# Loads of one input issued from ScalarE's queue, five load buffers and a new hand order in a gated linear-attention and token-mixing kernel

## Chip, cores and metric

The kernel runs on one core of one Trainium2 chip. The metric is the device time of one execution in microseconds. The names of the engines are those of the profile: PE is TensorE's matmul side, PEld its weight loads, DVE is VectorE, ACT is ScalarE, POOL is GpSimd, SP is SyncE, which issues most transfers. ACTq and SPq are the queues of DMA-issuing instructions of ScalarE and SyncE.

## What is computed

Inputs r, k, v, w are (4, 8, 768, 48) in float32: 4 batches, 8 heads, 768 steps, 48 columns. The first stage is a recurrence over the steps, per batch and head, with a 48 x 48 state that decays by w; the second mixes the tokens of a batch with weights made from their own projections.

```python
for t in range(S):
    cur = np.einsum('bhd,bhe->bhde', u[None] * kt, vt)
    y[:, :, t] = np.einsum('bhd,bhde->bhe', rt, state + cur)
    state = wt[:, :, :, None] * state + np.einsum('bhd,bhe->bhde', kt, vt)
x = y.transpose(0, 2, 1, 3).reshape(B, S, H * D)      # (4, 768, 384)
W_tok = scale * np.einsum('bsd,btd->bst', x @ w_q, x @ w_k)
out = np.maximum(np.einsum('bst,btd->bsd', W_tok, x), 0) @ w_out
```

## The kernel before

The work is cut into 12 units of 256 steps, three to a batch, and a unit into two chunks c of 128 steps. The recurrence is written in its chunked form. For a unit n the steps are, with the names of the tiles that the profile shows:

- Four loads of 384 KB each (wg, kg, rg, vg; `load`, line 222), all from SP's queue, each into one of four buffers that take turns.
- Decays: ScalarE takes the logarithm of wg (lw, line 379); PE sums it along the steps with a triangular matrix CM (cw); ScalarE makes two exponentials of the sums, ep (line 423) and en (line 428).
- k and r are cast to bfloat16 (line 389) and transposed on PE with the identity ID; the transposed k is copied (ks), the products are qT (line 462), RT = r x ep (line 471, VectorE) and KT = k x en (line 476, VectorE or GpSimd). v is cast in quarters into VB (line 493). Vd (line 515, GpSimd) is v times the bonus dd.
- Per chunk: PE multiplies RT and KT to a 128 x 128 matrix A for each head; VectorE masks it to AM (line 535, 24 in all). PE transposes KT (kb), which is copied to kd; PE adds kd x VB to the old state (sn), and VectorE scales it to the new state SB (line 602), four tiles in turn.
- PE multiplies AM with VB (ya) and RT with the old state (yi); VectorE or ScalarE writes the result plus Vd as X (lines 668 and 670).
- X is transposed to XT, on PE for most units, by a DMA transpose from SP's queue for units 9 and 10 (`TURN`), and projected to QK (wk and wq). After the third unit of a batch, X and QK give a 64 x 384 matrix T, copied to TS. For each of the batch's units PE multiplies QK with TS (mx), an engine takes the relu into MX (lines 271 and 273), PE multiplies with wo (fp), an engine copies to os (line 259 or 265), and a store leaves from SP's queue (line 803).

The first and the last unit are split: their en, ep, RT, KT, kb and kd, and for the last also X, XT, QK, MX and os, are made in two halves, one for each chunk, so that the second half need not be waited for.

No scheduler decides the order. Every step is entered in a plan (`Plan.add`) with the engines that it may run on. Three tables written out by hand then fix everything: `ORDER` is the order in which the steps are issued, `WAYS` the engine of each step with a choice, and `BANKS` the PSUM bank of each intermediate result. An engine works through its instructions in that order; semaphores for the tiles are set from it. Each load takes one of eight DMA semaphores in turn, in the order of the program, and waits until the load that had it before has landed. Steps of kind z are matmuls on a zero tile that only keep PE at work. The numbers of buffers are in `RINGS` (line 193). A slot of RT, KT, ep or en holds one pair of heads hp and one chunk c, 128 columns, at place 2 x hp + c, so that the halves of a split unit lie interleaved in one tile:

```python
def plain(t, cs=(0, 1)):
    return view(t, cs[0] * C, [[1, 1024]] if len(cs) > 1 else [[U, NP], [1, C]])
```

All code below runs inside the function that sets up the tiles.

Of the kernel before, what the change touches and what calls it, by code (L numbers as in the profile page):

```python
# [32 lines left out]
class Plan:  # L33
# [86 lines left out]
]  # L120
WAYS = (
    "PPDDPDDDPDPDDPPPPPPDDPAPPEDddPPDAAcENDEDDAPEDdPAAEAEcEAEDAPPEDdAPAEDcNDEAAAAAAAADPPEAdPP"
    "AEAEEEAEDAPAcDPPADEAEcEAEAAPPcDdPPAEDcEAEADAAAAAAAPPcDdPPDEDccNDEAAPPcAdPPAeAEcNDEDAPPcD"
    "PPPDEDcEAEAAAADADAAPAcAdPPAEDEENDDPPcAdPPDeDccNDAPPcDPPPPDPPAcNDeAADNDEDDAADDDDDDAADAADN"
    "NNNNEEENNENNNENEEEENNEN"
)
# [16 lines left out]
def kernel(  # L143
# [12 lines left out]
    nc = tc.nc  # L156
# [703 lines left out]
```

## Time and profile before

| | |
|---|---|
| time, median of 3 runs (lowest, highest) | 101.48 us (100.37, 104.27) |
| time of the profiled execution | 99.53 us |
| its span, first to last instruction | 97.8 us |
| busy: PE, PEld, DVE, ACT, POOL | 87.7, 67.6, 81.7, 76.0, 68.1 us |
| granted clock of TensorE | 1.0 throughout |
| read, written | 19.66 MB, 4.72 MB |
| loads of 384 KB: from issue to landing, median by tile | 5.1 to 6.0 us |

The profiled execution lasts 1.73 us longer than its span; that is what lies before the first and after the last instruction. All times in the trace are counted from the start of the span. A row of a group names the line, engine, operation, output and inputs, and then the busy time in us, the mean duration of one in ns, the idle time of the engine just before, and what ended it. A row of a timeline has the start and the duration in us first; several alike are put together with their number behind an x, and the idle time before them stands in brackets. Two instructions that follow each other on VectorE or ScalarE overlap by some hundredths of a microsecond, so that they follow at a slightly shorter distance than their durations.

### The profile page before, as it was taken

The numbers are of one execution on the slowest core, as the hardware profiler recorded it, in microseconds if no ns is written. First come the engines' busy times: TensorE is split into PE (matmuls) and PEld (weight loads), VectorE is DVE, ScalarE is ACT, GpSimd is POOL, SyncE is SP. The second block draws the span as 40 slices with busy tenths as digits, with TensorE's granted clock in tenths as the row PEclk, the third lists the DMA queues.
The fourth block names the chain that finished last, engine by engine and source line by source line (L and its number), as shares of the span: only waits on it lengthen the run. The fifth ranks groups of instructions, "written<-read, shape, count | busy, mean of one in ns | idle before, by whom it ended". The sixth has DMA issues, their size and how long they took to land.

```text
span 97.8 us, 4074 instructions
## 1 busy us (share of the span) xinstructions
PE 87.7 (90%) x1710; PEld 67.6 (69%) x1713; DVE 81.7 (83%) x142; ACT 76.0 (78%) x112; POOL 68.1 (70%) x106
## 2 busy tenths in 40 slices
PE   4996888999889899999999999999999999998940
PEld 1354677878677798877788787897787776675410
DVE  5608989999999998999898999899998996384850
ACT  5237988889799799899999999869889856806610
POOL 6659758728799998767999998999968991000000
PEclk9999999999999999999999999999999999999999
DMA  1999999999999999999999999999913695928593
GB/s 29 304 323 325 325 325 299 222 292 315 287 306 247 227 287 215 304 270 245 303 301 308 277 300 294 311 323 248 289 57 132 195 153 150 397 83 322 215 319 112
DMA packets 54914, 25.03 MB, mean 256 GB/s; under 512 B 52592, under 2 KB 53744, under 8 KB 54896
## 3 DMA queue, kind: packets, MB, share of 16 engines
q1 hardware_dynamic: 54736, 24.58, 90.6%
q8 instruction: 13, 0.21, 0.8%
q10 hardware_dynamic: 160, 0.20, 0.6%
q14 instruction: 5, 0.04, 0.1%
HBM read 19.66 MB, written 4.72 MB: 249 GB/s over the span
## 4 chain that ended last, share of the span: by engine, by line
PE 42%; DMA 18%; POOL 18%; DVE 8%; issue 4%; ACT 3%; SPq 3%; POOLq 0%; DVEq 0%; ACTq 0%
PE PS L176 42%; DMA vg<-in_v_dram 12%; POOL VB L493 7%; POOL Vd L515 6%; DMA kg<-in_k_dram 6%; SPq L223 3%; DVE os L265 2%; POOL k L389 2%; POOL KT L476 2%; POOL r L389 2%; DVE RT L471 1%; ACT en L428 1%; DVE AM L535 1%; ACT ep L423 1%; DVE qT L462 1%
## 5 line engine op out<-in xcount | busy, mean ns | idle before, releaser
L535 DVE TENSOR_TENSOR AM<-PS,US 128x1024 bf16<-128x1024 f32 x24 | 28.8, 1218 | 1.0 <-PE PS L176 0.6
L493 POOL CAST VB<-vg 64x384 bf16<-64x384 f32 x42 | 21.1, 503 | 3.2 <-DMA vg<-in_v_dram 0.9
L515 POOL TENSOR_TENSOR Vd<-VB,dd 128x768 bf16<-128x768 bf16 (+1 forms) x14 | 18.0, 1292 | 1.6 <-DVE dd L265 1.1
L428 ACT ACTIVATE en<-PS,km 128x1024 bf16<-128x1024 f32 (+1 forms) x14 | 13.6, 989 | 2.4 <-PE PS L176 2.0
L423 ACT ACTIVATE ep<-PS,kp 128x1024 bf16<-128x1024 f32 (+1 forms) x14 | 13.8, 1003 | 1.4 <-PE PS L176 1.1
L176 PE MATMUL PS<-wo,MX 128*128 128x384 bf16 x72 | 13.5, 326 | 0.5 <-DVE MX L273 0.5
L176 PEld LDWEIGHTS <-KT 48*128 48x128 bf16 (+1 forms) x288 | 10.3, 95 | 3.9 <-issue 1.7
L389 POOL CAST k<-kg 128x768 bf16<-128x768 f32 x11 | 9.0, 824 | 4.5 <-DMA kg<-in_k_dram 4.3
L379 ACT ACTIVATE lw<-wg 128x768 bf16<-128x768 f32 x12 | 10.1, 844 | 2.2 <-DVE kd L230 2.1
L176 PE MATMUL PS<-RT,KT 48*128 48x128 bf16 x192 | 9.2, 217 | 1.2 <-DVE qT L462 0.5
L176 PE MATMUL PS<-CM,lw 64*128 64x128 bf16 (+1 forms) x160 | 9.4, 230 | 0.6 <-DVE ks L265 0.4
L176 PEld LDWEIGHTS <-MX 128*128 128x128 bf16 x72 | 6.2, 97 | 4.9 <-DVE MX L273 1.3
L476 DVE TENSOR_TENSOR KT<-PS,en 128x1024 bf16<-128x1024 bf16 (+1 forms) x10 | 6.3, 631 | 3.7 <-ACT en L428 3.6
L389 POOL CAST r<-rg 128x768 bf16<-128x768 f32 x10 | 8.2, 823 | 1.2 <-DMA rg<-in_r_dram 1.1
L271 ACT ACTIVATE MX<-PS 128x768 bf16<-128x768 f32 (+1 forms) x10 | 7.6, 780 | 1.5 <-PE PS L176 1.4
L471 DVE TENSOR_TENSOR RT<-PS,ep 128x1024 bf16<-128x1024 bf16 (+1 forms) x14 | 8.4, 610 | 0.5 <-PE PS L176 0.3
L462 DVE TENSOR_TENSOR qT<-PS,ks 128x1024 bf16<-128x1024 bf16 x12 | 8.2, 680 | 0.7 <-PE PS L176 0.7
L176 PEld LDWEIGHTS <-lw 64*128 64x128 bf16 (+1 forms) x160 | 6.8, 96 | 2.3 <-issue 0.9
L670 DVE TENSOR_TENSOR X<-PS,Vd 128x768 bf16<-128x768 f32 (+1 forms) x8 | 6.8, 850 | 1.6 <-PE PS L176 1.5
L176 PE MATMUL PS<-ID,r 128*128 128x128 bf16 x96 | 7.4, 220 | 0.8 <-POOL r L389 0.7
L176 PE MATMUL PS<-Z 128*128 128x512 bf16 x16 | 6.5, 523 | 1.2 <-DVE Z L826 1.2
L259 ACT COPY os<-PS 128x768 f32<-128x768 f32 (+1 forms) x9 | 6.2, 694 | 1.8 <-PE PS L176 1.8
(77 smaller groups left out, 189.7 us busy)
## 6 DMA issues: line engine op xcount, KB each, us to landing
wg<-in_w_dram SPq DMA_DIRECT2D x12, 384.0 KB, 5.3
kg<-in_k_dram SPq DMA_DIRECT2D x12, 384.0 KB, 6.0
rg<-in_r_dram SPq DMA_DIRECT2D x12, 384.0 KB, 5.1
vg<-in_v_dram SPq DMA_DIRECT2D x12, 384.0 KB, 5.9
out_dram<-os SPq DMA_DIRECT2D x9, 384.0 KB, 2.6
out_dram<-os SPq DMA_DIRECT2D x5, 192.0 KB, 2.6
wof<-in_moe_w_out_dram SPq DMA_DIRECT2D x1, 576.0 KB, 6.2
out_dram<-os ACTq DMA_DIRECT2D x1, 192.0 KB, 2.3
```

The costliest lines, as they stand in the source:

```text
L176: return nc.tensor.matmul(o, l, rr, start=start, stop=stop, skip_group_check=True, is_transpose=trans)
L271: nc.scalar.activation(o, i, ACT.Relu)
L379: nc.scalar.activation(view(lw.tile, 0, [[64, H], [512, 2], [1, D]]), view(g["wg"].tile, 0, [[D2, H], [D, 2], [1, D]]), ACT.Ln, bias=0.0, ...
L389: op(view(o.tile, 0, [[64, H], [512, 2], [1, D]]), view(g[src].tile, 0, [[D2, H], [D, 2], [1, D]]))
L423: nc.scalar.activation(view(ep.tile, cs[0] * EW + 1, [[2 * EW, NP], [EW, len(cs)], [1, C]]), sums(cs), ACT.Exp, bias=kp, scale=1.0)
L428: nc.scalar.activation(view(en.tile, cs[0] * C, [[U, NP], [C, len(cs)], [1, C]]), sums(cs), ACT.Exp, bias=km, scale=-1.0)
L462: lambda e: nc.vector.tensor_tensor(qT.tile, at(rt, BF16), ks.tile, ALU.mult),
L471: nc.vector.tensor_tensor(slots(RT.tile, cs, C, 0, 64), slots(at(rt, BF16), cs, C, 0, 64), slots(ep.tile, cs, EW, 65, -65), ALU.mult)
L476: on("D" if e == "d" else e).tensor_tensor(plain(KT.tile, cs), plain(at(kt, BF16) if e == "d" else ks.tile, cs), plain(en.tile, cs), ALU.mult)
L493: op(view(VB.tile, c * DM, [[1, DM]], p0=half * 64, pn=64), view(g["vg"].tile, (1 - half) * D, [[D2, H], [1, D]], p0=c * 64, pn=64))
L515: (nc.vector if e == "D" else nc.gpsimd).tensor_tensor(Vd.tile[:, cols], VB.tile[:, cols], view(dd.tile, cs[0] * H, [[1, len(cs) * H], [0, ...
L535: AMs[c] = add(("AM", n, c), "D", lambda e, c=c, A=A: nc.vector.tensor_tensor(view(AM[c].tile, 0, [[C, 8], [1, C]]), view(at(A), 0, [[C, 8 ...
```

## The change

- `load` may issue from ScalarE's queue, and does so for wg of units 5 to 11: seven of the 48 loads. In the order, the load of unit n comes after the logarithm of unit n - 3.
- The four load tiles have five buffers each instead of four.
- In the first and the last unit, chunk comes first in the tiles: place c x 4 + hp instead of 2 x hp + c, so that each half lies in one piece. Each half of kb gets a bank of its own (in a split unit it had a half of one), and in the last unit the halves of MX lie apart.
- The two DMA transposes come after all loads of the last unit in the order.
- `ORDER`, `WAYS` and `BANKS` are new throughout; of each, the diff shows the first line. PE has 3408 instructions that the order lists instead of 3428, DVE 151 instead of 144, ACT 122 instead of 117, POOL 106 instead of 111, SP 62 instead of 69.

```diff
 ORDER = [
-    36, 37, 38, 39, 83, 84, 85, 124, 86, 126, 125, 180, 22, 21, 17, 9, 5, 19, 13, 23, 24, 16,
+    36, 37, 38, 83, 84, 39, 85, 86, 180, 124, 126, 125, 6, 32, 13, 14, 15, 18, 7, 0, 16, 1, 10,
...
 TURN = (9, 10)
+OWN = 5
...
-        wg=(4, HW, F32), rg=(4, HW, F32), kg=(4, HW, F32), vg=(4, HW, F32), os=(10, 2 * DM, F32),
+        wg=(5, HW, F32), rg=(5, HW, F32), kg=(5, HW, F32), vg=(5, HW, F32), os=(10, 2 * DM, F32),
...
     def load(b, i, tl, ap, e):
-        nc.sync.dma_start(
+        (nc.scalar if e == "A" else nc.sync).dma_start(
...
         fine = each if split else both
+        hp_s, c_s = (1, NP) if split else (2, 1)
+
+        def slot(hp, c):
+            return hp * hp_s + c * c_s
...
-            g[name + "L"] = dma((name, n), lambda e, ap=ap, x=g[name].tile: load(b, i, x, ap, e),
+            g[name + "L"] = add((name, n), "A" if name == "wg" and n >= OWN else "S",
+                                lambda e, ap=ap, x=g[name].tile: load(b, i, x, ap, e),
                                 buf=g[name])
+
+        if end:
+            for x in turned_x:
+                x["after"] += [g[z + "L"] for z in ("wg", "kg", "rg", "vg")]
+
+        if n >= OWN:
+            g["wgL"]["after"].append(lns[n - 3])
...
         def plain(t, cs=(0, 1)):
-            return view(t, cs[0] * C, [[1, 1024]] if len(cs) > 1 else [[U, NP], [1, C]])
+            return view(t, cs[0] * 512, [[1, 512 * len(cs)]])
...
-        kb, kd = either() if len(fine) == 1 else bank(), ring("kd")
+        kd = ring("kd")
         kds = {}
         for cs in ([(0,)] if final else fine):
-            def f_kb(e, cs=cs):
+            kb = bank() if split else either()
+
+            def f_kb(e, cs=cs, kb=kb):
...
-                    e, view(MX.tile, cs[0] * C, [[64, 2], [U // len(cs), NK * len(cs)], [1, 64]]),
+                    e, view(MX.tile, cs[0] * DM, [[64, 2], [C, NK * len(cs)], [1, 64]]),
```

More of the change, by code (lines that the diff above doesn't have):

```diff
@@ L84 @@
 ORDER = [
[35 rows of a table removed]
[35 rows of a table added]
 ]
 WAYS = (
[L122 to L125, printed above, removed]
+    "DDDPDDDDPDDPPDDPDDADDPAPPEDddPADAAEcEAEAAAPcDdPPDEDEEEAEAAPAEDdPPAEAEEAEDAAAAAADAPPEDdAP"
+    "DEAEcNDEDAPPEDPPPDEAcEEAEDAPPEDdPPDEAcNDEAAAADADAAAPcDdPAAeDEENDEDAPPcAPPPAEAEENDEDDPPcA"
+    "dPPDEAcNDEAADDAAAAAPPcAPPPDEDccNDDPPcAPPPAeDccNDAPAcDPPPPDPPAENDeDDDNDeADDDAADAAADDDDDAE"
+    "EENEEEENENNENNNNNNENENN"
 )
 BANKS = [
[7 rows of a table removed]
[7 rows of a table added]
 ]
@@ L359, in bonus @@
                        reads=[z])
+    turned_x = []
+    lns = []
     def unit(n, batch):
@@ L382, in unit @@
         ln = add(("ln", n), "A", f_ln, [g["wgL"]], lw, [g["wg"]])
+        lns.append(ln)
         def cast16(name, src, ways):
@@ L423, in f_ep @@
                 nc.scalar.activation(
-                    view(ep.tile, cs[0] * EW + 1, [[2 * EW, NP], [EW, len(cs)], [1, C]]),
+                    view(ep.tile, cs[0] * c_s * EW + 1,
+                         [[hp_s * EW, NP], [c_s * EW, len(cs)], [1, C]]),
                     sums(cs), ACT.Exp, bias=kp, scale=1.0)
@@ L428, in f_en @@
                 nc.scalar.activation(
-                    view(en.tile, cs[0] * C, [[U, NP], [C, len(cs)], [1, C]]), sums(cs), ACT.Exp,
+                    view(en.tile, cs[0] * c_s * C, [[hp_s * C, NP], [c_s * C, len(cs)], [1, C]]),
+                    sums(cs), ACT.Exp,
                     bias=km, scale=-1.0)
@@ L531, in f_A @@
                         mm(x[:, ds(hh * 512 + hp * C, C)],
-                           KT.tile[ds(hh * 64, D), ds((2 * hp + c) * C, C)],
-                           RT.tile[ds(hh * 64, D), ds((2 * hp + c) * C, C)])
+                           KT.tile[ds(hh * 64, D), ds(slot(hp, c) * C, C)],
+                           RT.tile[ds(hh * 64, D), ds(slot(hp, c) * C, C)])
             As = add(("A", n, c), "E", f_A, [RTs[c], KTs[c]], A, [RT, KT], mode=1)
@@ L556, in unit, with f_kd @@
                     [KTs[c] for c in cs], kb, [KT], cols=len(cs), mode=dict(e=1, E=0))
-            def f_kd(e, cs=cs):
+            def f_kd(e, cs=cs, kb=kb):
                 n4 = NP * len(cs)
                 if kb.kind == "s":
-                    x = view(at(kb, BF16), cs[0] * 512, [[C, n4], [64, 2], [1, D]])
+                    x = view(at(kb, BF16), 0, [[C, n4], [64, 2], [1, D]])
                 else:
-                    x = view(at(kb, BF16), cs[0] * NP * D, [[D, n4], [1024, 2], [1, D]])
+                    x = view(at(kb, BF16), 0, [[D, n4], [1024, 2], [1, D]])
                 copy(e, view(kd.tile, 64 + cs[0] * 1024, [[256, n4], [128, 2], [1, D]]), x, UNIT)
@@ L619, in f_yi @@
                     nc.tensor.drain()
[L620 removed]
+                mm(of(c, 2 * hp + hh), RT.tile[ds(hh * 64, D), ds(slot(hp, c) * C, C)],
                    olds[c].tile[ds(hh * 64, D), ds(hp * D, D)],
@@ L701, in unit @@
                     [xs], XT, [X])
+                turned_x.append(XTs)
             else:
@@ L790, in f_fp @@
                             mm(at(fp)[:, ds(c * 512, DM)],
-                               MX.tile[:, ds(kt * U + c * C, C)],
+                               MX.tile[:, ds((c * NK + kt if end else 2 * kt + c) * C, C)],
                                wo_sb[:, ds(kt * DM, DM)], start=(kt == 0), stop=(kt == NK - 1))
```

13 lines of the change are left out of this document (6 added, 7 removed), and 82 rows, old and new, of tables (BANKS, ORDER).

## The prediction

> **What bounds the kernel now.** I first read the busy shares of the page, then the windows before and after VectorE's last mask multiply (AM, line 535, 24 of them). The columns of a window row are the busy time, with instructions, of PE, PEld, DVE, ACT and POOL, the granted clock, the DMA share and GB/s.
>
> ```profile
> PE 87.7 (90%) x1710; PEld 67.6 (69%) x1713; DVE 81.7 (83%) x142; ACT 76.0 (78%) x112; POOL 68.1 (70%) x106
> 6.62:75.30 68.68, 64.26 (x1415) 53.55 (x1417) 64.73 (x104) 62.46 (x91) 58.47 (x79) 1.00 1.02 275
> 10.43:80.33 69.90, 66.52 (x1498) 55.74 (x1501) 66.72 (x106) 63.00 (x91) 59.92 (x79) 1.00 0.99 263
> 80.33:97.80 17.47, 13.09 (x161) 7.82 (x158) 9.39 (x18) 7.65 (x15) 0.82 (x2) 1.00 0.64 232
> ```
>
> The run has two parts. From the first mask (10.43) to the end of the last (80.33) VectorE works 66.72 of 69.90 us: 3.2 us idle, so its own work sets the pace. PE is as full, but its ends are modelled. ScalarE from its first en to its last ep (6.62 to 75.30) has 62.46 of 68.68 us, 6.2 idle. After 80.33 nothing is full: VectorE is busy for 9.39 of 17.47, and the end is a chain. I read that chain from VectorE's timeline and PE's:
>
> ```profile
> 79.10 1.23 DVE L535 TENSOR_TENSOR AM<-PS,US 128x1024 bf16<-128x1024 f32 x1
> 82.58 0.36 DVE L602 TENSOR_TENSOR SB<-PS,ep 128x192 bf16<-128x192 f32 x1 [0.35 <-PE PS L176]
> 84.51 0.37 PE L176 MATMUL PS<-VB,AM 128*128 128x48 bf16 x8
> 84.99 0.56 DVE L670 TENSOR_TENSOR X<-PS,Vd 128x384 bf16<-128x384 f32 x1 [1.49 <-PE PS L176]
> 89.84 1.49 DVE L273 TENSOR_SCALAR MX<-PS 128x384 bf16<-128x384 f32 x3 [1.01 <-PE PS L176]
> 93.57 1.04 DVE L265 COPY os<-PS 128x384 f32<-128x384 f32 x2 [0.29 <-PE PS L176]
> ```
>
> The last mask is done at 80.33, but the matmul that uses it (VB,AM) starts at 84.51, because in PE's order the last state (SB, 82.58) and its readers stand first. From 84.51 to the end of the span are 13.3 us: 5.3 to the first relu (MX), 4.8 to the last output copy (94.6), 3.2 for the store and the close.
>
> **The change, term 1: what VectorE must do up to the last mask.** VectorE, last rows, before:
>
> ```order
> L602 TENSOR_TENSOR SB_2_121<-PS_62,ep_0_97 128x192
> L535 TENSOR_TENSOR AM0_1_116<-PS_62,US_147 128x1024
> L670 TENSOR_TENSOR X_1_130<-PS_62,Vd_0_113 128x2x8x48
> L265 COPY dd_1_112<-PS_62 128x16
> L535 TENSOR_TENSOR AM1_1_118<-PS_62,US_147 128x1024
> L670 TENSOR_TENSOR X_1_130<-PS_62,Vd_1_114 128x384
> L265 COPY os_2_81<-PS_62 128x768
> L602 TENSOR_TENSOR SB_3_122<-PS_62,ep_1_98 128x192
> L265 CAST QK_1_132<-PS_62 128x256
> ```
>
> and in the change:
>
> ```order
> L482 TENSOR_TENSOR qT_1_108<-PS_62,ks_1_106 128x1024
> L491 TENSOR_TENSOR RT_1_110<-PS_62,ep_1_102 128x512
> L266 COPY os_3_86<-PS_62 128x768
> L623 TENSOR_TENSOR SB_3_126<-PS_62,ep_1_102 128x192
> L266 COPY dd_1_116<-PS_62 128x16
> L555 TENSOR_TENSOR AM1_1_122<-PS_62,US_151 128x1024
> L555 TENSOR_TENSOR AM0_1_120<-PS_62,US_151 128x1024
> L691 TENSOR_TENSOR X_1_134<-PS_62,Vd_1_118 128x384 x2
> ```
>
> The last state update (SB_3) has moved ahead of both last masks, and both halves of X follow the masks at once. Counted from the first mask to the last, VectorE now has more to do; the prices:
>
> ```profile
> L265 DVE COPY os<-PS 128x768 f32<-128x768 f32 x3 | 2.9, 950 | 0.3 <-PE PS L176 0.3
> L670 DVE TENSOR_TENSOR X<-PS,Vd 128x768 bf16<-128x768 f32 x6 | 5.7, 947 | 0.0
> L265 DVE COPY XT<-PS 128x768 bf16<-128x768 bf16 x4 | 2.2, 548 | 0.1
> L602 DVE TENSOR_TENSOR SB<-PS,ep 128x192 bf16<-128x192 f32 x20 | 7.0, 348 | 0.3 <-PE PS L176 0.3
> L265 DVE COPY dd<-PS 128x16 f32<-128x16 f32 x6 | 1.0, 168 | 0.8 <-PE PS L176 0.8
> L267 DVE TENSOR_SCALAR kd<-PS 128x768 bf16<-128x768 bf16 x3 | 1.6, 546 | 0.0
> L267 DVE TENSOR_SCALAR kd<-PS 128x384 bf16<-128x384 bf16 x3 | 1.0, 347 | 0.0
> L476 DVE TENSOR_TENSOR KT<-PS,en 128x1024 bf16<-128x1024 bf16 x8 | 5.5, 682 | 0.4 <-ACT en L428 0.3
> L265 DVE CAST QK<-PS 128x256 bf16<-128x256 f32 x3 | 1.2, 415 | 0.1
> L265 DVE COPY os<-PS 128x384 f32<-128x384 f32 x3 | 1.6, 557 | 0.8 <-ACT os L259 0.5 <-PE PS L176 0.3
> ```
>
> Added: two os (1.90), one X (0.95), one XT (0.55), one SB (0.35), two dd (0.34), one whole kd (0.55), and two that VectorE did not run in this size: a whole relu MX (nearest row os of 768, 0.95; lowest bound XT, 0.55) and a TS of 384 (between QK 0.42 and os of 384, 0.56: 0.5). Removed: two KT (1.36, to GpSimd), three half kd (1.04, to ScalarE), one QK (0.42). Sum 6.09 - 2.82 = **+3.3 us**. That work was in the tail or on other engines before. If nothing else changed, the last mask would end at 83.6.
>
> **Term 2: idle time of VectorE in that part.** Five load buffers let loads run a unit further ahead, and 7 of the 48 big loads leave SP's queue, where one that waits for its buffer holds all behind it. Little of VectorE's 3.2 us idle hangs on loads, though: most waits above end on PE. I take 1.0 back, bounds 0 and 2.5.
>
> **Term 3: issuing on ScalarE.** ScalarE, from the Ln (lw) of unit 7 to the next exponentials, before (a wait on DMAHW is on one of eight semaphores that all loads take in turn):
>
> ```order
> L379 ACTIVATE lw_1_92<-wg_3_66 128x8x2x48 [waits DMAHW1_49]
> L259 CAST QK_1_132<-PS_62 128x256 [waits PE_49]
> L259 COPY ks_1_102<-PS_62 128x1024 [waits DVE_49,PE_49]
> L428 ACTIVATE en_1_100<-PS_62,km_150 128x1024 [waits PE_49]
> L423 ACTIVATE ep_1_98<-PS_62,kp_149 128x8x128
> ```
>
> and in the change, where the loads of w for units 8 and 9 follow:
>
> ```order
> L396 ACTIVATE lw_1_96<-wg_2_65 128x8x2x48 [waits DMAHW2_49,Activation_49]
> L224 DMA wg_3_66<-in_w_dram 128x8x96 [waits DMAHW1_49]
> L224 DMA wg_4_67<-in_w_dram 128x8x96 [waits DMAHW3_49]
> L260 CAST QK_0_135<-PS_62 128x256 [waits DVE_49,PE_49]
> L260 CAST QK_0_135<-PS_62 128x256
> L441 ACTIVATE ep_1_102<-PS_62,kp_153 128x8x128 [waits DVE_49,PE_49]
> ```
>
> So QK, ep and en, which PE and VectorE need, now queue behind two issues and their semaphores. The trace has no large issue on ScalarE; the nearest are SP's own (start, duration) and ScalarE's two tiny ones:
>
> ```profile
> 0.79 0.46 SPq L223 DMA_DIRECT2D wg<-in_w_dram  x1
> 1.30 0.57 SPq L223 DMA_DIRECT2D kg<-in_k_dram  x1
> 3.01 1.15 SPq L223 DMA_DIRECT2D vg<-in_v_dram  x1
> 3.03 0.83 ACTq L289 DMA_DIRECT2D uR<-in_u_dram  x2
> wg<-in_w_dram SPq DMA_DIRECT2D x12, 384.0 KB, 5.3
> ```
>
> A first issue on an empty queue takes 0.46, the second 0.57, later ones on SP's full queue 1.15. ScalarE's queue holds at most two loads: five issues at 0.46 and two, the second of a pair, at 0.57 are **3.4 us**; the upper bound is 7 x 1.15 = 8.1. Besides, from first en to last ep ScalarE loses X, XT, r and a whole kd and gets k, wo and three half kd:
>
> ```profile
> L668 ACT CAST X<-PS 128x768 bf16<-128x768 f32 x5 | 4.0, 800 | 0.6 <-PE PS L176 0.5
> L259 ACT COPY XT<-PS 128x768 bf16<-128x768 bf16 x5 | 3.9, 809 | 0.2 <-PE PS L176 0.2
> L389 ACT CAST r<-rg 128x768 bf16<-128x768 f32 x2 | 1.6, 820 | 0.0
> L261 ACT ACTIVATE kd<-PS 128x768 bf16<-128x768 bf16 x4 | 3.2, 803 | 0.3 <-PE PS L176 0.3
> L389 ACT CAST k<-kg 128x768 bf16<-128x768 f32 x1 | 0.9, 855 | 0.0
> L265 POOL CAST wo<-wof 128x1152 bf16<-128x1152 f32 x1 | 1.1, 1148 | 0.0
> L261 ACT ACTIVATE kd<-PS 128x384 bf16<-128x384 bf16 x3 | 1.4, 489 | 1.2 <-PE PS L176 1.2
> ```
>
> -3.23 + 3.47 is +0.2 (wo at GpSimd's price; its QK more and two dd less cancel). So 3.6 us go into 6.2 of idle: most is covered, but such holes are small and the issues stand at fixed places, so I let 0.3 us reach the masks. With no cover it would be 3.6.
>
> **Term 4: from the last mask to the end.** With SB and its readers done before, VB,AM follows the last mask within 0.1 us: the 4.2 us between 80.33 and 84.51 go. Behind it PE gets two turned units' wk and wq, which were in front before, and one wo group less:
>
> ```profile
> 83.94 0.35 PE L176 MATMUL PS<-wk,XT 128*128 128x64 bf16 x6
> 84.22 0.36 PE L176 MATMUL PS<-XT,wq 128*64 128x128 bf16 x6
> 84.73 1.14 PE L176 MATMUL PS<-wo,MX 128*128 128x384 bf16 x6
> ```
>
> A wk with its wq takes 0.57 from start to start (83.94 to 84.51), a wo group 0.97 (84.73 to 85.70): with six more small matmuls, QK,TS, at wk's pace (0.28) that is 1.14 + 0.28 - 0.97 = +0.4 or a little more. In the last 4.8 us VectorE had five half relus (1.49 for three) and three copies (0.557 each), 4.2 us, ScalarE far less; now VectorE has two and four (3.2), and ScalarE four relus and two copies: about -0.8. The halves in their own tiles and banks (KT, RT, kb, MX) leave instruction counts as they were; I price them at nothing, hidden by in-order neighbours, with up to 0.3 gained if a reader waited for the other half. The tail is 0.1 + 13.3 + 0.4 - 0.8 = **13.0 us**.
>
> **Sum.** Last mask 80.3 + 3.3 - 1.0 + 0.3 = 82.9; end of span 95.9 against 97.8. The profiled run took 99.53, 1.73 beyond its span: 97.6. The median shown, 101.48, is 1.95 above the profiled run, and I carry that: **99.6 us**, 1.9% faster. The cover of the whole gain is narrow: +3.3 on VectorE against -4.2 and -0.8 behind it.
>
> **Rivals.**
> *VectorE loses most of its idle time.* For: GpSimd's casts, whose results feed everything, wait for loads (page: k 4.3 us of idle):
>
> ```profile
> L389 POOL CAST k<-kg 128x768 bf16<-128x768 f32 x11 | 9.0, 824 | 4.5 <-DMA kg<-in_k_dram 4.3
> ```
>
> Against: it has slack elsewhere. VectorE keeps 0.7 of its 3.2 idle and ScalarE's issues are covered: the last mask at 81.1, span 94.1, time 97.8, 3.6% faster.
>
> *ScalarE becomes the bound (slower).* Each issue costs 1.15 on ScalarE as on SP, and only 2 of the 8.1 us fall into idle time. Then the last ep ends 6.3 us later than the 75.30 of the window, at 81.6. In the order, r of the last unit, a relu, an output copy and kd stand between that ep and SB (r 0.82, two of the size of X and XT at 0.80, kd 0.49: with their overlap 2.6), then PE's sn, dps and A (three groups the size of VB,AM at 0.37: 1.1) and two masks (2.4): 6.1 us, last mask 87.7, span 100.7, time 104.4, 2.9% slower. It decides as soon as the last ep is later than 76.8. For it: a rule of the Trainium skill, "Perfetto Trace Analysis", section "DMA Instruction — HWDGE (DVE, Sync)": a sequencer that issues must first lock the descriptor generator, which the queues share, and holds it until all descriptors are made. By it ScalarE would wait out whatever SP is issuing, and an estimate is half of 1.15 + 0.46 each, 7.2 us in all. Against: ScalarE's two tiny issues finished within 0.83 us from 3.03 while SP's vg was being issued from 3.01 to 4.16, so the lock was not held through.
>
> *The queues wait for each other.* SP's queue in the change, from the load of k for unit 8 on:
>
> ```order
> L224 DMA kg_3_76<-in_k_dram 128x8x96 [waits DMAHW0_49]
> L224 DMA vg_2_80<-in_v_dram 128x8x96 [waits DMAHW1_49]
> L224 DMA vg_3_81<-in_v_dram 128x8x96 [waits DMAHW2_49,Activation_49,Pool_49]
> L224 DMA rg_4_72<-in_r_dram 128x8x96 [waits DMAHW3_49,Pool_49]
> L224 DMA kg_0_73<-in_k_dram 128x8x96 [waits DMAHW4_49,Pool_49]
> ```
>
> DMAHW1 is what ScalarE's load of w for unit 8 (wg_3_66) signals, so SP's load of v for unit 7 (vg_2_80), and all behind it, now waits until that w has landed; before, SP's loads waited for SP's own. The same v and its cast, before:
>
> ```profile
> 43.34 1.25 SPq L223 DMA_DIRECT2D vg<-in_v_dram  x1
> 45.84 0.85 ACT L379 ACTIVATE lw<-wg 128x768 bf16<-128x768 f32 x1
> 50.55 2.14 POOL L493 CAST VB<-vg 64x384 bf16<-64x384 f32 x4
> ```
>
> That w is issued behind the Ln of unit 7, which ran at 45.84, and lands up to 5.3 us later; even with that Ln 2 us earlier, v would start near 49.5 instead of 43.34, and VB near 53.5 instead of 50.55. GpSimd has little slack there: 3 us, last mask 85.9, span 98.9, time 102.6, 1.1% slower.
>
> **How the numbers follow.** Forecast 0.48, VectorE's idle 0.20, ScalarE bound 0.17, queues 0.15. A measurement of this kernel tells about 2% from no change. The forecast lies on that line and gives 0.22 to faster, 0.25 to same, 0.01 to slower; the queues give 0.11 to same and 0.04 to slower; ScalarE's bound gives 0.02 to same and 0.15 to slower: faster 0.42, same 0.38, slower 0.20. The forecast's own range, by terms 2 and 3, is 97.5 to 102; with the rivals, 96.2 to 104.0.
>
> **What would show it.** Right: the seven ACTq loads at 0.4 to 0.6 us each; the last AM ending at 82 to 84; VB,AM at once behind it; span minus last mask near 13. Wrong: ACTq issues of 1 us and more with ep and en late behind them; SP's v load after 48; a tail above 14.5.

## The result, and the profile after

The changed kernel takes 104.73 us (median of 4 runs, 104.01 to 105.66) where the kernel before took 100.93 (4 runs, one more than in the table above, 100.14 to 104.27): ratio 1.038, 95% interval 1.027 to 1.049. Run once more, in a later session, it took 102.58 (102.27 to 103.27) against 101.11: 1.016 (1.008 to 1.023). So it is slower, by 1 to 5%, where 99.6 us had been forecast. Runs of one kernel scatter by some per cent; the medians here are over all runs, the ratios compare only runs within 1.5% of the fastest of their kernel.

The profiled execution of the changed kernel took 105.08 us, with a span of 103.3. Nothing in the engines' busy times explains 5.5 us more of span (before: PE 87.7, DVE 81.7, ACT 76.0):

```profile
PE 89.2 (86%) x1701; PEld 68.8 (67%) x1703; DVE 83.2 (81%) x149; ACT 75.6 (73%) x110; POOL 69.9 (68%) x101
```

The loss has to be idle time, and the way to find it is to cut both runs at the same points of the work. VectorE's masks are good marks: I cut at the first mask, at the first mask of unit 4, at that of unit 8 and at the end of the last. The windows of the kernel before (columns as in the prediction; its tail is the row from 80.33 shown there):

```profile
10.43:33.66 23.23, 20.63 (x429) 17.51 (x432) 22.77 (x37) 20.47 (x30) 17.84 (x22) 1.00 1.06 283
33.66:60.40 26.74, 26.16 (x632) 22.16 (x633) 25.17 (x42) 25.62 (x36) 24.13 (x33) 1.00 1.07 283
60.40:80.33 19.93, 19.73 (x443) 16.06 (x440) 18.78 (x29) 16.90 (x27) 17.95 (x25) 1.00 0.82 212
```

and of the changed kernel, the first row being the whole stretch from the first mask to the last:

```profile
10.83:89.22 78.39, 71.14 (x1525) 59.11 (x1526) 70.07 (x110) 63.51 (x91) 64.76 (x83) 0.98 0.89 244
10.83:36.70 25.87, 20.91 (x422) 17.43 (x423) 21.47 (x35) 21.00 (x29) 18.57 (x26) 1.00 1.08 288
36.70:65.90 29.20, 27.13 (x624) 23.19 (x620) 26.28 (x41) 24.79 (x37) 25.88 (x34) 0.94 1.00 276
65.90:89.22 23.32, 23.10 (x491) 18.49 (x487) 22.32 (x36) 17.72 (x27) 20.31 (x24) 1.00 0.53 153
89.22:103.30 14.08, 10.02 (x133) 6.09 (x129) 7.20 (x16) 6.34 (x12) 0.00 (x0) 1.00 0.66 247
```

Two things are to be seen. **The moved work cancels.** The last part has grown by 3.39 us and the tail has shrunk by 3.39: both together take 37.40 us in either kernel. PE's busy time falls by 3.07 us in the tail (13.09 to 10.02) and rises by 3.37 in the last part, where PE is busy for 23.10 of 23.32 us (19.73 of 19.93 before): the work that came out of the tail is paid in full. **The loss lies before.** The first part is 2.64 us longer and the middle part 2.46, though VectorE has no more to do in them (47.75 us against 47.94). With 0.4 us until the first mask that is the 5.5.

What stands still there? SP's queue first (list of waits: us in total, times, the longest):

```profile
SPq L224 <- DMA wg<-in_w_dram: 5.7, 2, 4.9
```

In the timelines of SP, ScalarE and PE the same looks so:

```profile
36.91 1.46 SPq L224 DMA_DIRECT2D kg<-in_k_dram  x1
43.32 0.37 SPq L224 DMA_DIRECT2D vg<-in_v_dram  x1
...
50.38 3.90 SPq L224 DMA_DIRECT2D vg<-in_v_dram  x2
```

```profile
22.29 1.11 ACT L447 ACTIVATE en<-PS,km 128x1024 bf16<-128x1024 f32 x1
22.30 1.03 ACTq L224 DMA_DIRECT2D wg<-in_w_dram  x2
...
36.45 0.38 ACTq L224 DMA_DIRECT2D wg<-in_w_dram  x1
...
44.55 0.41 ACTq L224 DMA_DIRECT2D wg<-in_w_dram  x1
45.00 0.59 ACTq L224 DMA_DIRECT2D wg<-in_w_dram  x1
```

```profile
57.57 0.62 PE L177 MATMUL PS<-ID,k 128*128 128x128 bf16 x8 [1.72 <-POOL k L407]
```

ScalarE issues w of unit 7 at 36.45. SP's load of v for unit 6 has the same DMA semaphore one turn later and starts at 43.32, 4.9 us after the queue was free (before: 38.52, from the timeline there). All loads behind it slip. The one that PE feels is r of unit 8: it is issued at 45.50, right behind ScalarE's two loads at 44.55 and 45.00, and is under way for 8.9 us, until 54.4. GpSimd's timeline has its cast next:

```profile
54.48 0.82 POOL L407 CAST r<-rg 128x768 bf16<-128x768 f32 x1 [1.73 <-PE PS L177]
```

(The profile names PE as what ended this wait, but PE's last transposes of r had ended at 53.23; the load came last.) The cast of k stands behind that of r, and so PE stands for 1.72 us before the transposes of k for unit 8. Then the clock halves. Windows from the end of that wait on, the granted clock in the third column from the right:

```profile
58.40:59.20 0.80, 0.80 (x38) 0.76 (x36) 0.37 (x2) 0.80 (x1) 0.71 (x3) 1.00 1.09 301
59.20:60.00 0.80, 0.80 (x19) 0.60 (x14) 0.80 (x1) 0.28 (x2) 0.74 (x2) 0.50 0.67 164
60.00:61.00 1.00, 1.00 (x16) 0.73 (x15) 1.00 (x3) 1.00 (x2) 0.94 (x2) 0.50 0.97 265
...
63.00:64.00 1.00, 1.00 (x34) 0.86 (x32) 0.97 (x2) 1.00 (x3) 0.96 (x3) 1.00 0.96 336
```

For some 3.4 us PE runs at half speed, which is 1.7 us of its work lost. Before, all of it was granted 1.00.

### The profile page after: what moved, and what is told of

Read it like the earlier page. It is cut to its first block, busy times and chain, and to the rows that moved or that the text cites. A ratio compares the mean times of both kernels' runs of the same rounds, so it can differ in the third digit from the quotient of the medians.

```text
span 103.3 us, 4060 instructions
## 1 busy us (share of the span) xinstructions
PE 89.2 (86%) x1701; PEld 68.8 (67%) x1703; DVE 83.2 (81%) x149; ACT 75.6 (73%) x110; POOL 69.9 (68%) x101
## 4 chain that ended last, share of the span: by engine, by line
PE 50%; SPq 22%; POOL 11%; DMA 8%; issue 4%; DVE 1%; POOLq 0%
PE PS L177 50%; SPq L224 22%; DMA rg<-in_r_dram 8%; POOL Vd L535 3%; POOL k L407 2%; POOL VB L513 2%; POOL r L407 2%; POOL KT L496 1%; DVE MX L274 1%; DVE os L266 1%; POOLq L407 0%
## 5 line engine op out<-in xcount | busy, mean ns | idle before, releaser
L496 POOL TENSOR_TENSOR KT<-ks,en 128x1024 bf16<-128x1024 bf16 (+1 forms) x6 | 10.8, 1806 | 0.6 <-PE PS L177 0.4
L407 POOL CAST k<-kg 128x768 bf16<-128x768 f32 x10 | 8.2, 824 | 2.4 <-DMA kg<-in_k_dram 2.2
L177 PE MATMUL PS<-ID,k 128*128 128x128 bf16 x96 | 7.8, 227 | 2.1 <-POOL k L407 1.9
L623 DVE TENSOR_TENSOR SB<-PS,ep 128x192 bf16<-128x192 f32 x20 | 7.0, 352 | 2.4 <-PE PS L177 2.2
```

The lines of the kernel that those rows point to most:

```text
L177: return nc.tensor.matmul(o, l, rr, start=start, stop=stop, skip_group_check=True, is_transpose=trans)
L407: op(view(o.tile, 0, [[64, H], [512, 2], [1, D]]), view(g[src].tile, 0, [[D2, H], [D, 2], [1, D]]))
L496: on("D" if e == "d" else e).tensor_tensor(plain(KT.tile, cs), plain(at(kt, BF16) if e == "d" else ks.tile, cs), plain(en.tile, cs), ALU.mult)
```

## The experiments

The rival theories: **A**, the two queues hold each other up; **B**, the new order of the engines' work is slow by itself; **C**, the clock; and from the second group on **D**, what counts is the order in which the loads arrive. The table has the parts, cut as above in each kernel's own profile ("to 0" ends at the first mask). They are those of one execution each, which took 101.24 us for x11, 101.34 for x13 and 105.53 for x15.

| kernel | time, median (range) | ratio to before (95%) | to 0 | first | middle | last | tail |
|---|---|---|---|---|---|---|---|
| before | 100.93 (100.14-104.27) | | 10.43 | 23.23 | 26.74 | 19.93 | 17.47 |
| changed | 104.73 (104.01-105.66) | 1.038 (1.027-1.049) | 10.83 | 25.87 | 29.20 | 23.32 | 14.08 |
| x0 changed, again | 102.58 (102.27-103.27) | 1.016 (1.008-1.023) | 10.08 | 25.92 | 26.78 | 23.87 | 14.15 |
| x2 before, 5 buffers | 101.27 (99.64-105.59) | 0.999 (0.991-1.008) | 10.54 | 22.95 | 26.55 | 20.36 | 17.50 |
| x3 before, w from ScalarE | 102.12 (102.08-102.65) | 1.026 (1.021-1.030) | 10.96 | 24.48 | 27.28 | 20.74 | 17.44 |
| x6 changed, old places | 103.54 (102.69-104.85) | 1.023 (1.008-1.038) | 10.66 | 24.45 | 29.35 | 23.31 | 14.23 |
| x7 changed, PE kept busy | 102.87 (102.68-103.73) | 1.034 (1.027-1.040) | 10.16 | 24.89 | 27.81 | 23.90 | 14.14 |
| x4a w7 sooner | 101.93 (101.59-102.55) | 1.009 (1.001-1.017) | 10.02 | 24.71 | 27.35 | 23.64 | 14.18 |
| x4b w7 to w11 sooner | 102.78 (101.91-103.68) | 1.034 (1.023-1.045) | 10.05 | 24.82 | 27.27 | 23.90 | 14.16 |
| x15 w5, w6 on SP | 103.46 (100.82-105.53) | too few alike | 10.22 | 22.90 | 31.71 | 24.94 | 14.03 |
| x8 w5, w6 on SP, rest sooner | 103.96 (103.55-104.67) | 1.033 (1.023-1.043) | 10.25 | 23.11 | 31.33 | 23.89 | 14.02 |
| x10 the same, w5 sooner | 103.47 (102.57-105.24) | 1.021 (1.012-1.030) | 10.03 | 22.37 | 30.56 | 23.87 | 14.07 |
| x1 all on SP | 106.91 (104.52-107.01) | too few alike | 10.24 | 23.23 | 34.35 | 23.32 | 13.96 |
| x11 all on SP, sooner | 102.77 (101.24-105.54) | 1.002 (0.993-1.012) | 10.10 | 22.38 | 29.07 | 23.96 | 13.99 |
| x12 before, light loads | 99.29 (99.17-131.11) | 0.990 (0.980-1.000) | | | | | |
| x13 changed, light loads | 99.22 (98.83-101.34) | 0.988 (0.978-0.999) | 10.51 | 25.14 | 26.12 | 23.69 | 14.14 |
| x14 as x11, light loads | 98.64 (98.12-98.78) | 0.983 (0.974-0.991) | 10.46 | 22.75 | 26.12 | 23.68 | 13.99 |

Read down the last two columns first: in every kernel with the new order the last part and the tail are the same within 0.7 us, but for one last part, of x15. All that differs lies before the first mask of unit 8.

In the edits of `ORDER` below, the loads of w for units 5 to 11 are the steps 261, 317, 357, 398, 454, 493 and 533; each is shown with the steps between which it stands.

**One part of the change at a time.** Five buffers alone, in the kernel before (x2):

```diff
-        wg=(4, HW, F32), rg=(4, HW, F32), kg=(4, HW, F32), vg=(4, HW, F32), os=(10, 2 * DM, F32),
+        wg=(5, HW, F32), rg=(5, HW, F32), kg=(5, HW, F32), vg=(5, HW, F32), os=(10, 2 * DM, F32),
```

> The kernel before with five buffers for each of the four load tiles instead of four, nothing else changed. In the kernel before, waits of SP for a free buffer hold later loads, and GpSimd's k waits 4.3 us for loads. If the buffers are what helps, 99 us; if the order was made for four, no change: within 0.7 us of the kernel before. Theories A and B both expect no loss here.

No change, 0.999 (0.991 to 1.008). The old places of the chunks in the changed kernel (x6), with `plain` and `slots` to match:

```diff
-        hp_s, c_s = (1, NP) if split else (2, 1)
+        hp_s, c_s = (2, 1)
```

> The changed kernel with the old, interleaved places of the chunks in the tiles of the first and the last unit (2 x hp + c); banks, order, queues and buffers as changed. I priced the new places at nothing, with up to 0.3 us gained: expected within 0.5 us of the changed kernel's 104.7. If the halves lying apart cost or save something in the tail, the time from the last mask to the end differs from 14.1 us.

103.54 us lies between the two measurements of the changed kernel, 102.58 and 104.73, and the tail has 14.23 us: no effect that can be seen. The loads of w from ScalarE's queue alone, in the kernel before (x3); their places in `ORDER` move as well, each right behind the Ln of unit n - 2:

```diff
-        nc.sync.dma_start(
+        (nc.scalar if e == "A" else nc.sync).dma_start(
...
-            g[name + "L"] = dma((name, n), lambda e, ap=ap, x=g[name].tile: load(b, i, x, ap, e),
+            g[name + "L"] = add((name, n), "A" if name == "wg" and n >= 5 else "S", lambda e, ap=ap, x=g[name].tile: load(b, i, x, ap, e),
```

> The kernel before with one part of the change alone: the loads of w for units 5 to 11 are issued from ScalarE's queue, each right behind the Ln of unit n - 2; order of all else and four buffers as before. Theory A: SP's loads wait for ScalarE's here too, with SP gaps of 3 us and more behind the loads of w, and the time is 102 to 105 us against 100.9. Theory B (order): within 1 us of the kernel before. If the issues as such cost ScalarE its time: every issue 0.4 us and more between two busy instructions, 7 of them 3 us, 103 to 104 without gaps of SP.

2.6% slower (2.1 to 3.0): this one part does as much harm as the whole change. Not in the way that theory A said, though: among the long waits of SP in its profile none ends on a load of w. The largest piece is in the first part, 24.48 us instead of 23.23: w of unit 5 is issued at 18.83 us (24.63 before), ahead of w of unit 4 at 21.09, and the Ln of unit 4 waits 1.06 us for its own w. Queue and place change together here, so this run does not tell the one from the other. The issues themselves took 0.37 to 0.45 us.

**The changed kernel again (x0), and its queues.**

> The changed kernel once more, so that the runs beside it are compared on one chip: 104.4 us, within 0.7.

2 us faster than the first time. SP is held just as long (its wait for w 6.9 us in sum, the longest 4.4), but PE's wait before k of unit 8 is 1.09 us, not 1.72, and the middle part is as short as before the change: r of unit 8 is under way for 7.3 us this time, not 8.9. What this execution loses, it loses in its first part: PE waits 1.53 us there for v of unit 3, and the clock is at 0.50 from 32.6 us on for 3.4 us. So the hold that I saw first goes with 2.5 us of the middle part in one execution and with nothing in another. Now only the load of w for unit 7 is moved, behind the Ln of unit 4 (224; x4a):

```diff
-    ... 246, 357, 270, ...
+    ... 224, 357, 152, ...
```

> The changed kernel with one load moved: w of unit 7 is issued on ScalarE's queue right behind the Ln of unit 4, near 28 us, instead of behind that of unit 6, at 36.5. Theory A, the queues hold each other up: SP's load of v for unit 6 no longer waits until 43.3, k of unit 8 comes earlier, PE's wait of 1.7 us for it and the half clock behind it go: the middle part, from the first mask of unit 4 to the first of unit 8, takes 27.3 to 28 us instead of 29.2, time 102.5 to 103.3. Theory B (order): no change, 104.4.

SP's long hold is gone (v of unit 6 starts at 38.77), the middle part takes 27.35 us, the time is 101.93 against 102.58 beside it. That is 0.65 us, and the intervals of the two ratios overlap. All of w7 to w11 sooner (x4b):

```diff
-    246, 357, 270    361, 398, 285    217, 454, 162    402, 493, 164    301, 533, 421
+    224, 357, 152    265, 398, 158    321, 454, 269    361, 493, 285    402, 533, 164
```

> The changed kernel with the loads of w for units 7 to 11 still on ScalarE's queue, but each issued right behind the Ln of unit n - 3, some 2 to 10 us earlier. Theory A (SP's loads stand behind ScalarE's loads that are issued too late): SP's gaps at 38 to 43 and 48 to 50 us shrink to under 2 us each, last mask at 85 to 87, time 101 to 103 us. Theory B (the new order is slow by itself): within 0.7 us of the changed kernel's 104.7. A third, D: what hurts is that the loads on ScalarE's queue overtake SP's (r of unit 4 took 8.2 us to land); then earlier is worse, 105 to 107.

102.78 us, and a ratio of 1.034 by the runs beside it: within what the changed kernel measured, so B fits as well as A. No hold, no half clock, middle part 27.27, and still 24.82 in the first part. Here my first theory fell: the hold of SP is real, and it is not the loss.

**The clock.** Seven more matmuls on the zero tile before the transposes of k of unit 8 (408; x7). They are steps z that the changed kernel leaves out, set to PE in `WAYS`:

```diff
-    ... 379, 381, 408, 346, ...
+    ... 379, 381, 641, 626, 621, 638, 632, 640, 628, 408, 346, ...
```

> The changed kernel with seven more matmuls on the zero tile (0.2 us apart each) right ahead of the transposes of k of unit 8, before which PE was idle for 1.72 us at 55.9; they add work that the output does not use. Theory C, the clock: the granted clock of 0.50 from 59.2 to 62.4 us comes from that idle time; with PE kept at work it stays at 1.0, PE's 1.7 us come back, time 103 us. Theory A alone (loads late, the slow clock falls into PE's slack): clock 1.0, but less than 0.7 us gained. If the clock is not set by that idle time: still 0.50 near 59 us, no gain.

The matmuls fill the wait (timeline of PE, where six of the seven are recorded), and the clock stays at 1.00:

```profile
54.12 1.68 PE L175 MATMUL PS<-Z 128*128 128x512 bf16 x6
55.64 0.61 PE L175 MATMUL PS<-ID,k 128*128 128x128 bf16 x8
```

```profile
56.00:58.00 2.00, 2.00 (x68) 1.81 (x66) 1.10 (x2) 1.38 (x2) 1.80 (x4) 1.00 0.98 235
58.00:60.00 2.00, 1.83 (x37) 1.63 (x36) 1.95 (x5) 2.00 (x3) 1.99 (x2) 1.00 1.08 287
```

That fits a half clock that comes from the idle time, but does not prove it: the wait that they fill is about 1.45 us here (54.19 to 55.64), and after waits of 1.41 and 1.44 us elsewhere the clock did not fall. The middle part takes 27.81 us where the first profile of the changed kernel had 29.20; yet the ratio, 1.034, is that of the changed kernel. The profiled executions of x4b and x7 have no half clock between the first mask and the last, and their kernels are still 3.4% behind. The clock makes a late load dearer in the executions in which it falls; it is not the cause.

**All loads on one queue.** My first such kernel (x1) put w of unit 9 too far back:

```diff
-OWN = 5
+OWN = 12
...
-    189, 261, 317    261, 317, 188    246, 357, 270    361, 398, 285    217, 454, 162
+    262, 261, 223    263, 317, 27     319, 357, 358    359, 398, 455    401, 454, 456
...
-    402, 493, 164    301, 533, 421
+    494, 493, 495    534, 533, 535
```

> The changed kernel with all 48 loads issued from SP's queue again; the seven loads of w for units 5 to 11 stand among SP's loads by the time of their need. Order of the engines, tiles and five buffers stay as changed. Theory A, the queues hold each other up: in the changed kernel SP issued nothing between 38.4 and 43.3 us, because its load of v for unit 6 waited for ScalarE's load of w for unit 7 to land, and again before 50.4. With one queue that goes: gaps of SP in this part under 2 us, idle time of ScalarE and GpSimd that ends on a load falls from 15 us to under 9, the last mask ends at 84 to 86 instead of 89.2, time 100 to 102 us. Theory B, the new order and VectorE's 3.3 us more of work are slow by themselves: 104 to 105.5 us, last mask at 88 to 90.

```profile
59.42 0.84 ACT L394 ACTIVATE lw<-wg 128x768 bf16<-128x768 f32 x1 [4.32 <-DMA wg<-in_w_dram]
```

ScalarE waits 4.32 us for it (timeline of ScalarE), and PE behind it. 106.91 us is the price of my placing and tells nothing on A or B. My second (x9) put it too far forward, ahead of the Ln of unit 4 (224), which uses the same buffer:

```diff
-    262, 261, 223    263, 317, 27     319, 357, 358    359, 398, 455    401, 454, 456
+    222, 261, 262    223, 317, 263    264, 357, 319    358, 398, 320    455, 454, 400
```

> The changed kernel with all loads on SP's queue once more, now each w one to four loads earlier than in the first such run, where w of unit 9 stood behind v of unit 8 and ScalarE waited 4.3 us for it at 59.4. Theory A: without a second queue nothing holds SP but full buffers; last mask at 84 to 86, time 100.5 to 102. Theory B (the new order and its 3.3 us of moved work are slow by themselves): 103.5 to 105. If SP's queue with 48 loads is the bound (it issued one in about 1.15 us): loads late everywhere, 103 and more, with waits on loads over 10 us in sum.

That Ln then waited 22.56 us, for w of unit 9, which it also read in place of its own. The 122.63 us (122.06 to 124.11) answer nothing; the table leaves them out. The third (x11) puts w5 and w6 where the kernel before has them, and w9 right behind the Ln of unit 4:

```diff
-    262, 261, 223    263, 317, 27     319, 357, 358    359, 398, 455    401, 454, 456
+    222, 261, 262    263, 317, 27     264, 357, 319    358, 398, 320    224, 454, 152
...
-    494, 493, 495    534, 533, 535
+    456, 493, 236    321, 533, 269
```

> All loads on SP's queue, w of units 5 and 6 at the places of the kernel before, those of units 7 to 11 one to four loads earlier than in the first run with one queue, but w of unit 9 behind the Ln of unit 4, whose buffer it takes. Theory D: the second queue is not needed if the order of the loads is right: first part 23.2, middle part 27 to 28, last 23.5, tail 14.1: time 100 to 101.5. If 48 loads are too many for one queue: loads of k, r and v come late from 40 us on, middle part 30 and more, 103 to 105.

1.002 (0.993 to 1.012): the new order, without the second queue, is as fast as the kernel before, in those executions that come near its best of 101.24 us; two of its four, at 104.1 and 105.5, don't. In the other two B costs nothing that can be seen; the light loads below test it in all. The first part takes 22.38 us. In between lie kernels with only w5 and w6 back on SP's queue. The first (x8) keeps the rest early on ScalarE's:

```diff
-OWN = 5
+OWN = 7
...
-    189, 261, 317    261, 317, 188
+    262, 261, 223    263, 317, 27
```

with w7 to w11 as in x4b.

> As the run with early loads of w on ScalarE's queue, but w of units 5 and 6 goes back to SP's queue, behind k of unit 5 and r of unit 5; w of units 7 to 11 stays on ScalarE's queue, right behind the Ln of unit n - 3. Theory D (loads on the second queue overtake those that SP has issued before and are needed first): in the run before v of unit 4 was late, ScalarE and GpSimd waited for it 2.2 and 1.7 us near 29 us, and VectorE was idle for 2.3 us at 30 to 35; that goes, the masks of unit 4 start near 33.5 instead of 34.9, last mask ends at 84.5, time 100.7 us. Theory B (the new order itself leaves VectorE idle there): no change, 102.2.

(The late load of that text was v of unit 3, not of unit 4.) The second (x10) has w5 one load sooner on SP's queue:

```diff
-    262, 261, 223
+    222, 261, 262
```

> Loads of w for units 5 and 6 on SP's queue at the places where the kernel before has them (behind r of unit 4 and r of unit 5), those of units 7 to 11 early on ScalarE's queue. In the last such run w of unit 5 stood one load later, ScalarE's Ln waited 3.0 us for it, PE 2.2 us, and the clock fell to half. Theory D (what counts is the order in which the loads arrive, since to 36 us the loads come as fast as they can): the part from the first mask to that of unit 4 takes 23.2 us as there, the middle part 27.3 as with early loads, the last 23.9 and the tail 14.2: span 98.8, time 100.5. Theory B (the new order costs by itself): 102 and more.

and the third (x15) edits nothing but w5 and w6 in the changed kernel:

```diff
-OWN = 5
+OWN = 7
...
-    189, 261, 317    261, 317, 188
+    222, 261, 262    263, 317, 27
```

> The changed kernel with one edit: w of units 5 and 6 goes back to SP's queue, behind r of unit 4 and r of unit 5; w of units 7 to 11 stays as late on ScalarE's queue as in the change. Theory D: the part from the first mask to that of unit 4 takes 22.4 to 23.2 us instead of 25.9 (in five kernels with these two loads on ScalarE's queue 24.5 to 25.9). Whether it helps the end: if the loads as a whole bound the first 62 us, the middle part gives it back, and the time stays at 102.5 to 103.5; if the two loads were the loss, 100 to 101.

The first part does what theory D said each time: 22.37 to 23.23 us in all six profiles with the new order and w5, w6 on SP's queue (x9 aside), 24.45 to 25.92 in all seven with these two issued from ScalarE at 21 to 23 us. One load shows why: v of unit 3, from SP's queue, issued beside them. First the changed kernel (second profile; from issue to landing, and ScalarE's timeline), then the kernel with one queue:

```profile
DMA to landing us min/median/max: 8.7/8.7/8.7
```

```profile
29.94 1.04 ACT L513 CAST VB<-vg 64x384 bf16<-64x384 f32 x2 [2.19 <-DMA vg<-in_v_dram]
```

```profile
26.83 1.04 ACT L511 CAST VB<-vg 64x384 bf16<-64x384 f32 x2
```

With two queues v is under way for 8.7 us and ScalarE waits 2.19 for it; with one it was issued at 21.41 and its cast starts at 26.83, waiting for nothing. The two loads of w that ScalarE issued beside it are used at 33 us and later. The other profiles say the same: v of unit 3 is under way for 7.5 to 8.7 us in the six with two queues and full loads, for 5.3 in x1 with one, and for 6.1 in x13 below, where the loads from unit 5 on, the two of w beside it among them, are halved and v of unit 3 is not. SP's issue of v is part of that, but not the whole: in x0 the issue took 2.72 us instead of the 1.48 of x11, in the first profile of the changed kernel 1.48 as well, and v was still 7.5 us under way. It is not the only load that suffers: in that first profile ScalarE's longest wait here, 1.37 us, is for w of unit 4, issued by SP just before.

Yet in the profiles of the three kernels between, the middle part gave all of it back, and more: 30.56 to 31.71 us, with other loads late and the clock at half behind them. (The execution of x15 with 31.71 is its longest; its shortest took 100.82 us.) In all three GpSimd stands for v of unit 4: 1.73 us in x15, 2.97 in x8 and 2.36 in x10. In x10 the profile names PE as what ended that wait, but the load, issued at 26.79, was under way for 6.7 us, until 33.49. The cast of k and PE's transposes stand behind it, and w of unit 6 is late as well (x10; GpSimd's timeline, ScalarE's, PE's, and windows):

```profile
33.57 1.06 POOL L511 CAST VB<-vg 64x384 bf16<-64x384 f32 x2 [2.36 <-PE PS L175]
```

```profile
37.26 0.84 ACT L394 ACTIVATE lw<-wg 128x768 bf16<-128x768 f32 x1 [2.56 <-DMA wg<-in_w_dram]
```

```profile
35.58 0.84 PE L175 MATMUL PS<-ID,k 128*128 128x128 bf16 x8 [2.03 <-POOL k L405]
```

```profile
36.00:37.00 1.00, 1.00 (x18) 0.75 (x17) 0.00 (x0) 0.00 (x0) 0.88 (x3) 0.50 0.53 115
...
39.00:40.00 1.00, 1.00 (x35) 0.95 (x34) 0.84 (x2) 0.49 (x2) 1.00 (x1) 0.88 1.17 324
```

**Light loads.** If a stall that is removed at one place comes back at another, is it the loads at all? I halved them, from unit 5 on, and left all else, in the kernel before (x12), the changed one (x13) and x11 (x14):

```diff
+        hn = H // 2 if b * NU + i >= 5 else H
...
-            out=view(tl, 0, [[D2, H], [1, D2]]),
-            in_=ap[b, :, ds(i * U, U)].rearrange("h (p j) d -> p h (j d)", j=2))
+            out=view(tl, 0, [[D2, hn], [1, D2]]),
+            in_=ap[b, ds(0, hn), ds(i * U, U)].rearrange("h (p j) d -> p h (j d)", j=2))
```

> The kernel before with the loads of units 5 to 11 cut to half: only heads 0 to 3 of r, k, v and w are loaded, and the other heads are worked on with what an earlier unit left in the buffer, so the output is not the reference's. All instructions of the engines stay. It shows what the loads cost the order of before. Theory D (loads bound the first 60 us of the new order, and hardly those of the old): 0 to 1.5 us faster than the kernel before. Theory B (order): the same.

> The changed kernel with the same cut: of units 5 to 11 only heads 0 to 3 are loaded, the rest is left from an earlier unit, so the output is not the reference's. If late loads are the whole of the loss (theories A and D), the first mask of unit 8 comes at 60 us or sooner, as in the kernel before, and the time is 98 to 100, within 0.7 of the light kernel before. If the order itself loses (B): 101 to 102, and over 1.2 us more than the light kernel before.

> The run with all loads on SP's queue and w sooner, with the same cut of the loads from unit 5 on (output not the reference's). If loads are the loss: 97.5 to 99.5, no different from the changed kernel with light loads. If the queue matters even with half the bytes, it is 1 us and more faster than that. B: 101 and more.

99.29, 99.22 and 98.64 us: with half the bytes the kernel before, the changed one and the one with one queue lie within 0.7 us of each other. (Of the first only the times are used; its profiled execution, 131 us with the clock at 0.57, is not comparable.) The changed kernel gains 3.4 us and more over its two measurements, the kernel before about 1.5. The windows of the third, from the first mask on:

```profile
10.46:33.21 22.75, 21.39 (x424) 17.53 (x423) 21.20 (x36) 20.55 (x29) 18.64 (x26) 1.00 1.05 279
33.21:59.33 26.12, 25.77 (x623) 22.10 (x618) 25.95 (x40) 24.43 (x37) 25.21 (x33) 1.00 0.78 205
59.33:83.01 23.68, 23.17 (x492) 18.63 (x487) 22.45 (x36) 17.79 (x27) 20.81 (x25) 1.00 0.21 59
```

In the middle part VectorE has 25.95 of 26.12 us: with the loads out of the way the new order runs without gaps. So the loss of the changed kernel is late loads. What its new order is worth without them is about the 0.7 us between the medians of the light kernels, which their intervals do not tell from nothing. (The loads of units 0 to 4 are whole in all three: in the profiled execution of x13 GpSimd waits 2.31 us for v of unit 2, and its first part is still 25.14.)

## Why the prediction was wrong

**Term 1, VectorE's work up to the last mask: right.** +3.3 us forecast; 66.72 to 70.07 is +3.35.

**Term 2, VectorE's idle time: this step failed.** The prediction said that "Little of VectorE's 3.2 us idle hangs on loads" and took 1.0 back, with bounds of 0 and 2.5: both on the side of a gain. Idle time from the first mask to the last is 78.39 - 70.07 = 8.3 us, 5.1 more instead of 1.0 less (6.9 us in the second profile). The argument looked at the waits that were there, and not at those that would come: from the first mask to 60 us the kernel before moved 283 GB/s without a break, and the changed one 288 and 276, which reads as loads that come as fast as they can and just in time; a change of their order that brings some forward then makes others late, as v of unit 3 and r of unit 8 above. Of the 7.4 us by which the span was missed (95.9 to 103.3), 5.8 are this term (8.3 instead of the 2.5 that terms 2 and 3 left), 1.1 the tail, and 0.4 the time to the first mask.

The Trainium skill states the point that was passed over: by its page "DMA: Bandwidth & Descriptors", section "Issuing engines are not separate DMA queues", transfers that different engines start run on the same 16 DMA engines and interleave, so that a second issuer saves issue time and no more. The runs agree with it: in the first part the changed kernel moved 288 GB/s from two queues, the kernel before 283 from one, and what the second queue did was to share that out anew, at the cost of w of unit 4 and v of unit 3.

**Term 3, the issues on ScalarE: the price was right, the cover better.** Seven issues took 0.37 to 0.60 us each (in the second profile one took 1.18). They did not even fill idle time: the two at 22.30 run beside an exponential that began at 22.29. ScalarE's busy time fell by 0.4 us.

**Term 4, the tail: 13.0 forecast, 14.1 measured.** PE's timeline:

```profile
88.98 0.36 PE L177 MATMUL PS<-VB,AM 128*128 128x48 bf16 x8
89.27 0.34 PE L177 MATMUL PS<-QK,TS 64*128 64x128 bf16 x6
89.55 0.37 PE L177 MATMUL PS<-VB,AM 128*128 128x48 bf16 x8
...
95.34 0.68 PE L177 MATMUL PS<-QK,TS 64*128 64x128 bf16 x18
96.34 3.23 PE L177 MATMUL PS<-wo,MX 128*128 128x384 bf16 x18 [0.32 <-DVE MX L274]
```

VB,AM of the last chunk does follow the mask at once (0.33 us after 89.22, with six small matmuls between, instead of 0.1). From it to the last QK,TS it takes 5.79 us; before, from 84.51 to 89.46 in PE's timeline, it was 4.95: +0.84 for the turned units' work where I had +0.4. From there to the end it is 7.96 us against 8.34: -0.38 where I had -0.8. What VectorE was spared there came through by half.

What the sum hid is that PE, which I called as full as VectorE, pays the same bill: the 3.4 us by which the tail got shorter came back in the last part, where PE has 3.4 us more of matmuls and is at work for 99% of the time. Loads do not explain that part: in x14, with light loads and the DMA share at 0.21, it takes 23.68 us too. The forecast's net gain of 1.9 us had no place to come from but terms 2 and 4.

**The rivals.** VectorE losing its idle time: the reverse happened. ScalarE as the bound: no; its issues cost nothing that can be seen, and none is seen to wait out SP's: the longest, 1.18 us from 21.59 in the second profile, ended while SP's issue of v (21.11 to 23.83) was still under way. The queues waiting for each other: the mechanism is there word for word, one load earlier than I looked (w of unit 7 holds v of unit 6), and its 102.6 us is what the second measurement gave, by luck: taking the hold away won no more than 0.65 us (x4a), which its interval doesn't tell from nothing, and the cause that the experiments support, one step before it, was in no rival: loads that overtake.

**What stays open.** Which late load ends which execution changes from run to run: the changed kernel took 104.7 us in one session and 102.6 in another, with the same hold. Why v of unit 4 is late in the three kernels between, how much of the 3.8 to 5.0 us that their middle parts lose against the kernel before is due to it, and whether an arrangement of full loads exists that brings the new order to the 98.6 us of light ones, was not settled. Nor are two waits of PE that the profile puts down to nothing ("issue": 0.74 us near 68 us in x3, 1.50 near 67 in x15).

## What to carry to other kernels

Where loads arrive just in time at a steady rate, a second issuing queue is no more bandwidth: it is a new order of arrival, and each load that it brings forward makes another late; ask which. Before counting work that is moved from the tail into a full part as hidden, look whether the engine that pays is the same, on every engine that is full there. And bound a term on idle time on both sides: a kernel whose waits are short has more to lose than to win.

## What the runs showed of the hardware

- **The clock of TensorE falls after short waits.** After idle times of PE of 1.53, 1.72, 1.90, 2.03, 2.20 and 2.55 us (x0, changed, x6, x10, x8, x15) the granted clock went to 0.50, at once or up to 2.1 us after PE was at work again, and stayed there for 3.4 us (twice that in x8); after 1.41, 1.44 and 1.50 us (x6, changed, x15) it did not. At 1.49 us it fell in x1 and not in x4b. The Trainium skill, "TensorE: Matmul & The Clock Gate", section "Part 1: The HAM clock gate", has the half clock set by a window of 3.4 us that runs free of the kernel, which fits the 3.4 us and the two outcomes at 1.49; but it names a whole idle window as the condition, and here less than half of one was enough.
- **A DMA issue of 384 KB on ScalarE's queue takes 0.37 to 0.65 us in most cases and runs beside ScalarE's own instruction,** even while SP issues (SP's own took 0.37 to 2.3 us each from 30 to 60 us in the changed kernel). The second of a pair took 1.18 us in x0 and 1.16 in x6, beside an issue of SP's of 2.72 and 2.23 us: issues on the two queues can lengthen each other.
